# Score and value products of a pair of heads, issued head by head in turn

## The chip, the cores and the metric

The kernel runs on one core of one Trainium2 chip. The core has five engines that this text names by the short names of the profile: TensorE (PE, and PEld for its weight loads), VectorE (DVE), ScalarE (ACT), GpSimd (POOL) and SyncE (SP). Each works off its own instructions, and semaphores let one wait for another. The metric is the device time of one execution in microseconds, the median of the runs.

## The reference

Attention over 8 batches and 8 heads, 576 rows of 64 values each, keeps the 32 largest scores of each row. Its output, read as 4608 tokens of 512 values, goes through a SoLU block. All is float32.

```
scores = scale * q @ k.T                        # [8, 8, 576, 576]
kth    = the 32nd largest score of each row
attn   = softmax(scores where scores >= kth, else -1e9)
x      = (attn @ v), heads side by side         # [4608, 512]
h      = x @ w_in                               # [4608, 1024]
solu   = h * softmax(h)
ln     = (solu - mean) / sqrt(var + 1e-6) * g_ln
out    = ln @ w_out                             # [4608, 512]
```

## The kernel before

Attention runs in 32 pairs of heads, four pairs to a batch. The 576 query rows of a pair make five steps: four chunks of 128 rows, each with one tile per head, and one chunk for the two tails of 64 rows, which share a tile. So a pair has nine tiles of 128 by 576 scores.

For each step `scores` (line 206) multiplies queries with keys. Queries and keys of both heads lie in one tile `qkT` with the head dimension on the partitions, head 0 on 0 to 63 and head 1 on 64 to 127. A head's 576 columns are made in two halves of 288, in one tile `s_ps` of two PSUM banks per head, from a pool of two such tiles (`ps_big`). ScalarE scales and evicts it to `S_sb` (line 231).

`topk_softmax` finds the 32 largest on VectorE with four MAX8 and three MATCH_REPLACE8 (lines 243 and 253); ScalarE makes the exponentials `E_sb` (line 250); VectorE masks and sums them into `P_sb` (line 257); GpSimd divides by the sum (line 266). `transpose_p` turns `P_sb` on TensorE (`tp_p`, `tp_pt`, lines 277 and 280), and ScalarE copies the result to `PTm`, one tile per head for the 512 main columns, or to `PTt` for the tails.

After a pair's last step `attn_v` (line 284) multiplies values with these: into `om` (64 by 512 per head, head 0 on output partitions 0 to 63, head 1 on 64 to 127, both in one bank) and into `ot` (64 by 64 per head). Each is a sum of five products: four with `vm`, 128 rows of values, and one with `vt`, the 64 tail rows. ScalarE copies `om` to `xTm` (line 306) and `ot` to `xTt` (line 307).

When the four pairs of a batch are done, its tokens go through the SoLU block in tiles of 128: `mm1` makes `h_ps` (eight products, from `ps_big` too), `solu_ln` works on VectorE (`hmax`, line 326, first), ScalarE and GpSimd, and `mm2` transposes (`tp_ln`) and makes `o_ps`. One such piece of work is taken per step from the list `todo`. The weights come as float64 and are turned to float32 in 16 chunks in the first steps.

The order of instructions on each engine is not the order of the code: a scheduler gives each instruction a place by its inputs, its buffers and its own estimate of durations. An engine then works strictly down its list; ScalarE's list, for instance, mixes evictions, exponentials and copies. What the change moves is thus seen only in the built order.

Of the kernel before, what the change touches and what calls it, by code (L numbers as in the profile page):

```python
# [8 lines left out]
F32 = mybir.dt.float32  # L9
# [6 lines left out]
P = 128  # L16
# [2 lines left out]


def from_float64(nc, p1, p2, dst, raw):
    """dst = the nearest float32 of the float64 whose bits raw holds, in three stages.

    Bits of an integer only go through bitwise operations, or through
    arithmetic that is exact in float32: the exponent field alone, and the
    mantissa in its upper 20 and its lower 32 bits, whose sum is rounded once
    to float32. Past float32's range it gives infinity or zero.
    """
    words = raw.bitcast(U32).rearrange("p (f w) -> p f w", w=2)
    lo, hi = words[:, :, 0], words[:, :, 1]  # L30
    ex = p2.tile([P, 512], I32, tag="ln", name="w_ex")
    mi = p1.tile([P, 512], U32, tag="sq", name="w_mi")
    mant = p2.tile([P, 512], F32, tag="solu", name="w_mant")

    nc.vector.tensor_scalar(
        out=ex, in0=hi.bitcast(I32), scalar1=0x7FF00000, scalar2=None, op0=ALU.bitwise_and
    )
    nc.vector.tensor_scalar(
        out=mi, in0=hi, scalar1=0xFFFFF, scalar2=None, op0=ALU.bitwise_and
    )  # L40
    nc.gpsimd.tensor_scalar(
        out=mant, in0=mi, scalar1=2.0**-20, scalar2=1.0, op0=ALU.mult, op1=ALU.add
    )
    nc.gpsimd.tensor_scalar(
        out=ex, in0=ex, scalar1=float(-896 << 20), scalar2=0.0, op0=ALU.add, op1=ALU.max
    )
    nc.gpsimd.tensor_scalar(
        out=ex, in0=ex, scalar1=float(255 << 20), scalar2=8.0, op0=ALU.min, op1=ALU.mult
    )
    yield  # L50
    nc.vector.scalar_tensor_tensor(
        out=mant, in0=lo, scalar=2.0**-52, in1=mant, op0=ALU.mult, op1=ALU.add
    )
    nc.gpsimd.tensor_tensor(out=mant, in0=mant, in1=ex.bitcast(F32), op=ALU.mult)
    yield
    nc.vector.scalar_tensor_tensor(
        out=dst.bitcast(U32), in0=hi, scalar=0x80000000, in1=mant.bitcast(U32),
        op0=ALU.bitwise_and, op1=ALU.bitwise_or,
    )
# [3 lines left out]
def kernel(  # L63
# [7 lines left out]
    moe_g_ln: bass.AP,  # L71
    out: bass.AP,
):
    """Attention runs in pairs of heads, one batch after the other.

    A head's 576 rows are loaded as 512 main rows, row 4p + t on partition p in
    chunk t, and 64 tail rows; queries and keys keep that order throughout, and
    the stores undo it. The tails of the two heads share one tile of 128 query
    rows. The attention output is made transposed, [(head, d), token], as the
    first matrix product of the second part takes it.  # L80
    """
    nc = tc.nc
    B, H, S, D = q.shape
    NTOK, DM = out.shape
    DFF = moe_w_in.shape[1]
    NM = 4
    SM = NM * P
    ST = S - SM
# [7 lines left out]
    raw = ctx.enter_context(tc.tile_pool(name="raw", bufs=3))  # L96
# [4 lines left out]
    ps_big = ctx.enter_context(tc.tile_pool(name="ps_big", bufs=2, space=PS))  # L101
# [8 lines left out]
    w_out = const.tile([P, NF, DM], F32, tag="w_out", name="w_out")  # L110
    g_rows = const.tile([NF, P], F32, tag="g_rows", name="g_rows")
    g_col = const.tile([P, NF], F32, tag="g_col", name="g_col")

# [1 line left out]

    w_wide = moe_w_in.dtype != F32
    w_chunks = []
# [14 lines left out]
    def load_w(n):  # L132
        dst, src, _ = w_chunks[n]
        if w_wide:
            w_raw[n] = raw.tile([P, 512], mybir.dt.uint64, tag="w_raw", name="w_raw")
            dst = w_raw[n]
        nc.sync.dma_start(out=dst, in_=src)

    def finish_w(n):
        """The chunk's three stages; the next chunk's load goes ahead of the first."""  # L140
        dst, _, c = w_chunks[n]
        if n + 1 < len(w_chunks):
            load_w(n + 1)
        if w_wide:
            yield from from_float64(nc, p1, p2, dst, w_raw.pop(n))
        if c is not None:
            # ln * g @ w_out: g is per row of w_out
            nc.gpsimd.tensor_scalar(
                out=dst, in0=dst, scalar1=g_col[:, c : c + 1], scalar2=1.0,
                op0=ALU.mult, op1=ALU.mult,  # L150
            )
# [1 line left out]
    w_open = []  # L153

    def weights_step(n):
        """One stage of each open chunk, the oldest first."""
        if n < len(w_chunks):
            w_open.append(finish_w(n))
        for g in list(w_open):
            if next(g, w_open) is w_open:  # L160
                w_open.remove(g)

# [1 line left out]

    pairs = [(b, hp) for b in range(B) for hp in range(NP)]
    st = [dict() for _ in pairs]
# [2 lines left out]
    def load(i):  # L169
        b, hp = pairs[i]  # L170
        hh = slice(2 * hp, 2 * hp + 2)
        for nm, src in (("q", q), ("k", k), ("v", v)):
            # one free dimension per chunk for what the tensor engine loads as weights
            dims, order = ([P, NM, 2, D], "p t h d") if nm != "v" else ([P, 2, NM, D], "p h t d")
            m = raw.tile(dims, F32, tag=nm + "m", name=nm + "m")
            t = raw.tile([ST, 2, D], F32, tag=nm + "t", name=nm + "t")
            nc.sync.dma_start(
                out=m, in_=src[b, hh, 0:SM, :].rearrange(f"h (p t) d -> {order}", t=NM)
            )
            nc.sync.dma_start(out=t, in_=src[b, hh, SM:S, :].rearrange("h p d -> p h d"))  # L180
            st[i][nm] = (m, t)
# [25 lines left out]
        d["PTt"] = p2.tile([P, NM + 1, 2 * ST], F32, tag="PTt", name="PTt")  # L207

    def scores(i, t):
        """Score rows of query chunk t (NM: the tails), scaled, on chip."""  # L210
        d = st[i]
        qkT = d["qkT"]
        tail = t == NM
        qs = slice(SM, S) if tail else slice(t * P, (t + 1) * P)
        big = []
        for h in range(2):
            s = ps_big.tile([P, 2, 512], F32, tag="big", name="s_ps")
            hd = slice(h * D, (h + 1) * D)
            rows = slice(h * ST, (h + 1) * ST) if tail else slice(0, P)
            for half in range(2):  # L220
                nc.tensor.matmul(  # L221
                    out=s[rows, half, 0:SH], lhsT=qkT[hd, 0, qs],
                    rhs=qkT[hd, 1, half * SH : (half + 1) * SH], start=True, stop=True,
                )
            big.append((s, rows))
        d["S", t] = []
        for h, (s, rows) in enumerate(big):
            if h == 0 or not tail:
                sb = p4.tile([P, S], F32, tag="S", name="S_sb")
                d["S", t].append(sb)  # L230
            nc.scalar.activation(  # L231
                out=sb[rows, :].rearrange("p (a s) -> p a s", a=2), in_=s[rows, :, 0:SH],
                func=AF.Copy, scale=scale,
            )
# [48 lines left out]
    def attn_v(i):  # L283
        b, hp = pairs[i]
        d = st[i]
        if hp == 0:
            xs["m", b] = p2.tile([P, NP, SM], F32, tag="xTm", name="xTm")
            if b % 2 == 0:
                xs["t", b // 2] = p2.tile([P, NP, 2 * ST], F32, tag="xTt", name="xTt")
        xm, xt = xs["m", b], xs["t", b // 2]  # L290
        vm, vt = d["v"]
        om = ps_o.tile([P, 512], F32, tag="o", name="om")
        ot = ps_o.tile([P, 512], F32, tag="o", name="ot")
        for h in range(2):
            hd = slice(h * D, (h + 1) * D)
            for o, n, rhs in (
                (om, SM, d["PTm"][h]),
                (ot, ST, d["PTt"][:, :, h * ST : (h + 1) * ST]),
            ):
                for c in range(NM + 1):  # L300
                    ks = P if c < NM else ST
                    nc.tensor.matmul(  # L302
                        out=o[hd, 0:n], lhsT=vm[:, h, c, :] if c < NM else vt[:, h, :],
                        rhs=rhs[0:ks, c, :], start=(c == 0), stop=(c == NM),
                    )
        nc.scalar.copy(out=xm[:, hp, :], in_=om)  # L306
        nc.scalar.copy(out=xt[:, hp, (b % 2) * ST : (b % 2 + 1) * ST], in_=ot[:, 0:ST])
        d.clear()

# [1 line left out]

    def mm1(d, x):
        h = ps_big.tile([P, 2, 512], F32, tag="big", name="h_ps")
# [80 lines left out]
                ],  # L394
            )

# [1 line left out]

    steps = [(i, t) for i in range(len(pairs)) for t in range(NM + 1)]

# [7 lines left out]
    def behind(n):  # L408
        i, t = steps[n]
        transpose_p(i, t)  # L410
        if t == NM:
            attn_v(i)
            b, hp = pairs[i]
            if hp == NP - 1:
                queue_batch(b)

    load(0)
    load(1)
    ahead(0)
    load_g()  # L420
    load_w(0)
    for n in range(len(w_chunks) + 2):
        todo.append(lambda n=n: weights_step(n))
# [42 lines left out]
```

## Time and profile before

| | |
|---|---|
| three runs, us | 2178.75, 2178.86, 2180.56 (median 2178.86) |
| span of the profiled execution | 2181.4 us |
| its own time beside the span | none is given apart from the span |
| VectorE busy | 1910.7 us, 88% |
| TensorE busy (matmuls) | 1701.3 us, 78% |
| ScalarE busy | 813.0 us, 37% |
| GpSimd busy | 396.5 us, 18% |

The profile is of one execution; its span is 2.5 us above the median of the runs. A matmul's end is modelled, so from TensorE one reads the starts: the distance from one start to the next is what an instruction costs in a dense run. "Idle before" is the time that an engine stood still ahead of an instruction, with what ended the wait behind the arrow. Start times count from the first instruction. In the timeline neighbours of one kind are merged, with their count behind the x.

### The profile page before, as it was taken

Reading aid. Unit: us, or ns where it says so; the run is one execution under the profiler, and the core shown is the slowest. Engines: PE = TensorE matmul, PEld = TensorE weight load, DVE = VectorE, ACT = ScalarE, POOL = GpSimd, SP = SyncE. Lnnn points to the kernel's source line nnn. Section 1 sums busy time; section 2 is a strip of 40 time slices with the busy share of each in tenths; the row PEclk is TensorE's granted clock in tenths of the full one; section 3 lists DMA queues with packets and bytes.
Section 4 is the critical chain, followed back from the end, with each engine's and each line's share of the span. In section 5 each row is a group of like instructions: output and inputs, shape, how many; then the busy total and the mean of one; then the engine's idle time right before and its main releaser. Section 6 shows DMA issues by size and latency. Waiting matters only on the chain.

```text
span 2181.4 us, 20118 instructions
## 1 busy us (share of the span) xinstructions
PE 1701.3 (78%) x5761; PEld 844.0 (39%) x5761; DVE 1910.7 (88%) x4600; ACT 813.0 (37%) x1598; POOL 396.5 (18%) x475
## 2 busy tenths in 40 slices
PE   4537679786898878797787878977687987878787
PEld 2223334343343434343343434434343443344333
DVE  6889989999889998999899998899989998999931
ACT  2223334343344433443343433334334443334322
POOL 6871111111111111111111111111111110111111
PEclk9956678786798877896788977978678987789699
DMA  4210000000000000000000000000000000000000
GB/s 122 74 34 17 17 17 21 21 22 17 6 26 21 21 17 21 12 27 17 17 21 21 21 12 16 27 16 21 17 16 16 26 21 17 5 11 10 0 10 15
DMA packets 96766, 47.44 MB, mean 22 GB/s; under 512 B 81800, under 2 KB 90000, under 8 KB 96656
## 3 DMA queue, kind: packets, MB, share of 16 engines
q1 hardware_dynamic: 91408, 36.72, 6.7%
q10 hardware_dynamic: 5248, 9.44, 1.2%
q8 instruction: 46, 0.75, 0.1%
q14 instruction: 64, 0.52, 0.1%
HBM read 36.70 MB, written 9.44 MB: 21 GB/s over the span
## 4 chain that ended last, share of the span: by engine, by line
PE 55%; DVE 29%; ACT 6%; issue 6%; POOL 4%; DMA 0%; SPq 0%; POOLq 0%; ACTq 0%; DVEq 0%
PE om L302 12%; PE o_ps L365 11%; DVE rest L253 11%; PE h_ps L316 11%; DVE m L243 10%; PE s_ps L221 9%; PE tp_p L277 5%; DVE P_sb L257 5%; PE ot L302 2%; PE tp_ln L359 2%; ACT S_sb L231 2%; PE tp_qk L201 1%; POOL P_sb L266 1%; ACT PTm L278 1%; DVE solu L334 1%
## 5 line engine op out<-in xcount | busy, mean ns | idle before, releaser
L243 DVE MAX8 m<-rest 128x8 f32<-128x576 f32 x864 | 656.4, 760 | 17.1
L221 PE MATMUL s_ps<-qkT 64*128 64x288 f32 (+1 forms) x1280 | 435.8, 547 | 188.9 <-ACT S_sb L231 160.5
L266 POOL TENSOR_SCALAR P_sb<-P_sb,rden 128x576 f32<-128x576 f32 x288 | 218.0, 757 | 1564.7 <-DVE rden L265 1442.9
L277 PE MATMUL tp_p<-ident,P_sb 128*128 128x128 f32 x1152 | 243.3, 348 | 238.7 <-POOL P_sb L266 231.1
L253 DVE MATCH_REPLACE8 rest<-m,rest 128x576 f32<-128x576 f32 x576 | 427.6, 742 | 0.0
L221 PEld LDWEIGHTS s_ps<-qkT 64*128 64x128 f32 (+1 forms) x1280 | 213.5, 225 | 366.6 <-ACT S_sb L231 216.9
L277 PEld LDWEIGHTS tp_p<-ident,P_sb 128*128 128x128 f32 x1152 | 162.3, 174 | 400.6 <-POOL P_sb L266 301.2
L231 ACT ACTIVATE S_sb<-s_ps 128x576 f32<-128x576 f32 (+1 forms) x320 | 204.6, 650 | 299.2 <-PE s_ps L221 134.3
L278 ACT COPY PTm<-tp_p 128x512 f32<-128x512 f32 x256 | 149.9, 586 | 399.5 <-PE tp_p L277 399.5
L365 PE MATMUL o_ps<-w_out,lnT 128*128 128x512 f32 x576 | 278.4, 640 | 3.3 <-ACT lnT L362 3.3
L257 DVE SCALAR_TENSOR_TENSOR P_sb<-S_sb,m,E_sb 128x576 f32<-128x576 f32 x288 | 233.6, 811 | 47.9 <-ACT E_sb L250 46.5
L250 ACT ACTIVATE E_sb<-S_sb,nmax 128x576 f32<-128x576 f32 x288 | 222.3, 772 | 123.2 <-DVE nmax L246 122.6
L302 PE MATMUL om<-PTm,vm 128*64 128x512 f32 x512 | 242.7, 608 | 1.5 <-ACT PTm L278 1.5
L316 PE MATMUL h_ps<-w_in,xTm 128*128 128x512 f32 x512 | 236.3, 603 | 4.0 <-ACT S_sb L231 2.8
L243 DVE MAX8 m<-S_sb 128x8 f32<-128x576 f32 x288 | 213.9, 743 | 16.0 <-ACT S_sb L231 16.0
L253 DVE MATCH_REPLACE8 rest<-m,S_sb 128x576 f32<-128x576 f32 x288 | 213.9, 743 | 0.0
L365 PEld LDWEIGHTS o_ps<-w_out,lnT 128*128 128x128 f32 x576 | 115.8, 206 | 146.1 <-issue 134.5
L326 DVE TENSOR_REDUCE hmax<-h_ps 128x1 f32<-128x1024 f32 x36 | 44.0, 1221 | 124.5 <-PE h_ps L316 124.5
L316 PEld LDWEIGHTS h_ps<-w_in,xTm 128*128 128x128 f32 x512 | 92.7, 192 | 104.6 <-issue 95.5
L302 PEld LDWEIGHTS om<-PTm,vm 128*64 128x64 f32 x512 | 63.5, 138 | 139.5 <-issue 123.7
L280 PE MATMUL tp_pt<-ident,P_sb 128*64 128x128 f32 x288 | 97.8, 339 | 0.0
L306 ACT COPY xTm<-om 128x512 f32<-128x512 f32 x32 | 18.7, 585 | 197.1 <-PE om L302 197.1
(66 smaller groups left out, 1319.0 us busy)
## 6 DMA issues: line engine op xcount, KB each, us to landing
qm<-in_q_dram SPq DMA_DIRECT2D x32, 256.0 KB, 3.7
km<-in_k_dram SPq DMA_DIRECT2D x32, 256.0 KB, 3.9
vm<-in_v_dram SPq DMA_DIRECT2D x32, 256.0 KB, 2.7
out_dram<-osb ACTq DMA_DIRECT2D x32, 256.0 KB, 2.2
w_raw<-in_moe_w_in_dram SPq DMA_DIRECT2D x8, 512.0 KB, 3.9
w_raw<-in_moe_w_out_dram SPq DMA_DIRECT2D x8, 512.0 KB, 3.4
qt<-in_q_dram SPq DMA_DIRECT2D x32, 32.0 KB, 2.2
kt<-in_k_dram SPq DMA_DIRECT2D x32, 32.0 KB, 2.3
```

Source lines behind the costliest of these rows:

```text
L221: nc.tensor.matmul(out=s[rows, half, 0:SH], lhsT=qkT[hd, 0, qs], rhs=qkT[hd, 1, half * SH : (half + 1) * SH], start=True, stop=True,)
L231: nc.scalar.activation(out=sb[rows, :].rearrange("p (a s) -> p a s", a=2), in_=s[rows, :, 0:SH], func=AF.Copy, scale=scale,)
L243: nc.vector.max(m, cur)
L250: nc.scalar.activation(out=e, in_=sb, func=AF.Exp, bias=nmax)
L253: nc.vector.match_replace(nxt, m, cur, NEG)
L257: nc.vector.scalar_tensor_tensor(out=pt, in0=sb, scalar=m[:, 7:8], in1=e, op0=ALU.is_ge, op1=ALU.mult, accum_out=den,)
L266: nc.gpsimd.tensor_scalar(out=pt, in0=pt, scalar1=rden, scalar2=1.0, op0=ALU.mult, op1=ALU.mult)
L277: nc.tensor.transpose(tp[:, c, :], pt[:, c * P : (c + 1) * P], ident)
L278: nc.scalar.copy(out=dst[:, 0:NM, :], in_=tp)
L302: nc.tensor.matmul(out=o[hd, 0:n], lhsT=vm[:, h, c, :] if c < NM else vt[:, h, :], rhs=rhs[0:ks, c, :], start=(c == 0), stop=(c == NM),)
L316: nc.tensor.matmul(out=h[:, half, :], lhsT=x[:, c, :], rhs=w_in[:, c, half * 512 : (half + 1) * 512], start=(c == 0), stop=(c == NP - 1),)
L365: nc.tensor.matmul(out=o, lhsT=lnT[:, c, :], rhs=w_out[:, c, :], start=(c == 0), stop=(c == NF - 1),)
```

## The change

In `scores` both heads' tiles are taken first; then the loop over the halves is the outer one and the loop over the heads the inner one. In `attn_v` the loop over the heads becomes the innermost: `om` of both heads first, product by product in turn, then `ot`. The number, the sizes and the operands of the products stay. The remaining lines of the diff replace comments by blank lines. Line numbers from `scores` on differ by one or two between the kernels (the value product is line 302 before and line 301 after).

```diff
         big = []
         for h in range(2):
-            s = ps_big.tile([P, 2, 512], F32, tag="big", name="s_ps")
-            hd = slice(h * D, (h + 1) * D)
             rows = slice(h * ST, (h + 1) * ST) if tail else slice(0, P)
-            for half in range(2):
+            big.append((ps_big.tile([P, 2, 512], F32, tag="big", name="s_ps"), rows))
+
+        for half in range(2):
+            for h, (s, rows) in enumerate(big):
+                hd = slice(h * D, (h + 1) * D)
                 nc.tensor.matmul(
                     out=s[rows, half, 0:SH], lhsT=qkT[hd, 0, qs],
                     rhs=qkT[hd, 1, half * SH : (half + 1) * SH], start=True, stop=True,
                 )
-            big.append((s, rows))
...
-        for h in range(2):
-            hd = slice(h * D, (h + 1) * D)
-            for o, n, rhs in (
-                (om, SM, d["PTm"][h]),
-                (ot, ST, d["PTt"][:, :, h * ST : (h + 1) * ST]),
-            ):
-                for c in range(NM + 1):
-                    ks = P if c < NM else ST
+
+        for o, n in ((om, SM), (ot, ST)):
+            for c in range(NM + 1):
+                ks = P if c < NM else ST
+                for h in range(2):
+                    rhs = d["PTm"][h] if n == SM else d["PTt"][:, :, h * ST : (h + 1) * ST]
                     nc.tensor.matmul(
-                        out=o[hd, 0:n], lhsT=vm[:, h, c, :] if c < NM else vt[:, h, :],
+                        out=o[h * D : (h + 1) * D, 0:n],
+                        lhsT=vm[:, h, c, :] if c < NM else vt[:, h, :],
                         rhs=rhs[0:ks, c, :], start=(c == 0), stop=(c == NM),
                     )
```

Since a scheduler places the instructions, the lists of all engines move. Three places are shown, each of before and of the change. Numbers in names are running numbers of tiles; `PTm0` and `PTm1` are the transposed attention of the two heads; sizes are partitions by columns of the output.

TensorE at the end of the third batch's last pair, about 804 to 821 us in the trace of before; first before:

```order
L302 MATMUL om_5830<-PTm0_5256,vm_4337 64x512 x4
L277 MATMUL tp_p_5740<-ident_82,P_sb_5651 128x128 x4
L280 MATMUL tp_pt_5746<-ident_82,P_sb_5651 64x128
L302 MATMUL om_5830<-PTm0_5256,vt_4338 64x512
L302 MATMUL om_5830<-PTm1_5257,vm_4337 64x512 x4
L302 MATMUL om_5830<-PTm1_5257,vt_4338 64x512
L316 MATMUL h_ps_5854<-w_in_89,xTm_4410 128x512 x5
L277 MATMUL tp_p_5821<-ident_82,P_sb_5724 128x128 x4
L280 MATMUL tp_pt_5827<-ident_82,P_sb_5724 64x128
L316 MATMUL h_ps_5854<-w_in_89,xTm_4410 128x512
L302 MATMUL ot_5831<-PTt_5258,vm_4337 64x64 x4
L302 MATMUL ot_5831<-PTt_5258,vt_4338 64x64
```

The same place in the changed kernel, from the first value product on:

```order
L301 MATMUL om_5830<-PTm0_5256,vm_4337 64x512
L316 MATMUL h_ps_5854<-w_in_89,xTm_4410 128x512 x2
L278 MATMUL tp_p_5740<-ident_82,P_sb_5651 128x128 x4
L281 MATMUL tp_pt_5746<-ident_82,P_sb_5651 64x128
L316 MATMUL h_ps_5854<-w_in_89,xTm_4410 128x512
L301 MATMUL om_5830<-PTm1_5257,vm_4337 64x512
L301 MATMUL om_5830<-PTm0_5256,vm_4337 64x512
L301 MATMUL om_5830<-PTm1_5257,vm_4337 64x512
```

And, after three more `om` rows of the same kind, from the last product with `vm` on:

```order
L301 MATMUL om_5830<-PTm1_5257,vm_4337 64x512
L301 MATMUL om_5830<-PTm0_5256,vt_4338 64x512
L301 MATMUL om_5830<-PTm1_5257,vt_4338 64x512
L223 MATMUL s_ps_5863<-qkT_5676 128x288 x2
L278 MATMUL tp_p_5821<-ident_82,P_sb_5724 128x128 x4
L281 MATMUL tp_pt_5827<-ident_82,P_sb_5724 64x128
L316 MATMUL h_ps_5854<-w_in_89,xTm_4410 128x512
L301 MATMUL ot_5831<-PTt_5258,vm_4337 64x64 x8
L301 MATMUL ot_5831<-PTt_5258,vt_4338 64x64 x2
L316 MATMUL h_ps_5854<-w_in_89,xTm_4410 128x512 x4
```

Head 0's five `om` products and head 1's five stood as two blocks; now one product of head 0 stands alone, and the other nine alternate behind the transposes of head 1. Three of the eight `h_ps` products stand ahead of them, and one head's scores (`s_ps_5863`) ahead of the tails' transposes. The `ot` products of both heads stand together by `vm` and `vt`.

VectorE at that batch's end, around the first operation that reads the new `h_ps`; before:

```order
L253 MATCH_REPLACE rest_5802<-m8_5796,S_sb_5704 128x576
L262 TENSOR_SCALAR rden_5792<-den_5790 128x1
L326 TENSOR_REDUCE hmax_5941<-h_ps_5854 128x1
L265 RECIPROCAL rden_5792<-rden_5792 128x1
L243 MAX m8_5804<-rest_5802 128x8
L253 MATCH_REPLACE rest_5806<-m8_5804,rest_5802 128x576
L330 TENSOR_SCALAR rs_5944<-rs_5944 128x1
L243 MAX m8_5808<-rest_5806 128x8
```

And in the changed kernel:

```order
L254 MATCH_REPLACE rest_5802<-m8_5796,S_sb_5704 128x576
L263 TENSOR_SCALAR rden_5792<-den_5790 128x1
L244 MAX m8_5804<-rest_5802 128x8
L266 RECIPROCAL rden_5792<-rden_5792 128x1
L254 MATCH_REPLACE rest_5806<-m8_5804,rest_5802 128x576
L244 MAX m8_5808<-rest_5806 128x8
L326 TENSOR_REDUCE hmax_5941<-h_ps_5854 128x1
L254 MATCH_REPLACE rest_5810<-m8_5808,rest_5806 128x576
```

`hmax_5941` stood behind `rden_5792`; now two MAX and one MATCH_REPLACE of the running top-k stand ahead of it, and the operations that follow from it come later.

ScalarE at the end of the batch's second pair, about 701 to 708 us in the trace of before; before:

```order
L231 ACTIVATE S_sb_4849<-s_ps_4844 128x576
L306 COPY xTm_4410<-om_4910 128x512
L307 COPY xTt_4411<-ot_4911 128x64
L342 ACTIVATE sq_4945,var_4946<-solu_4941,nmu_4942 128x1024
L231 ACTIVATE S_sb_4959<-s_ps_4953 128x576
L231 ACTIVATE S_sb_4961<-s_ps_4956 128x576
L250 ACTIVATE E_sb_4967<-S_sb_4847,nmax_4965 128x576
```

And in the changed kernel:

```order
L232 ACTIVATE S_sb_4849<-s_ps_4842 128x576
L342 ACTIVATE sq_4945,var_4946<-solu_4941,nmu_4942 128x1024
L306 COPY xTm_4410<-om_4910 128x512
L307 COPY xTt_4411<-ot_4911 128x64
L251 ACTIVATE E_sb_4967<-S_sb_4847,nmax_4965 128x576
L232 ACTIVATE S_sb_4959<-s_ps_4953 128x576
L232 ACTIVATE S_sb_4961<-s_ps_4954 128x576
```

The exponential `E_sb_4967` stood behind `sq_4945` and two evictions of scores; now it follows the copies of `om` and `ot` directly, and `sq_4945` has gone ahead of these.

## Rows read from the trace of the kernel before

**Rows 1.** The page, busy time, share of the span and instructions of each engine.

```profile
PE 1701.3 (78%) x5761; PEld 844.0 (39%) x5761; DVE 1910.7 (88%) x4600; ACT 813.0 (37%) x1598; POOL 396.5 (18%) x475
```

**Rows 2.** Waits of VectorE, 300 to 2080 us: total, times, longest (us).

```profile
DVE hmax L326 <- PE h_ps L316: 73.7, 24, 6.0
DVE P_sb L257 <- ACT E_sb L250: 45.9, 37, 3.6
```

**Rows 3.** Timeline, VectorE, one batch: start us, us, what [idle before, releaser].

```profile
627.29 0.82 DVE L257 SCALAR_TENSOR_TENSOR P_sb<-S_sb,m,E_sb 128x576 f32<-128x576 f32 x1 [1.10 <-ACT E_sb L250]
...
647.28 1.23 DVE L326 TENSOR_REDUCE hmax<-h_ps 128x1 f32<-128x1024 f32 x1 [2.55 <-PE h_ps L316]
...
708.34 0.98 DVE L257 SCALAR_TENSOR_TENSOR P_sb<-S_sb,m,E_sb 128x576 f32<-128x576 f32 x1 [3.03 <-ACT E_sb L250]
...
771.63 0.82 DVE L257 SCALAR_TENSOR_TENSOR P_sb<-S_sb,m,E_sb 128x576 f32<-128x576 f32 x1 [2.57 <-ACT E_sb L250]
...
823.46 1.23 DVE L326 TENSOR_REDUCE hmax<-h_ps 128x1 f32<-128x1024 f32 x1 [5.97 <-PE h_ps L316]
...
824.67 0.74 DVE L243 MAX8 m<-rest 128x8 f32<-128x576 f32 x1
```

**Rows 4.** Timeline, TensorE, 803.9 to 823.5 us.

```profile
803.97 3.65 PE L302 MATMUL om<-PTm,vm 128*64 128x512 f32 x8
807.55 0.66 PE L277 MATMUL tp_p<-ident,P_sb 128*128 128x128 f32 x4
...
808.24 1.07 PE L302 MATMUL om<-PTm,vt 64*64 64x512 f32 x2
809.24 3.65 PE L302 MATMUL om<-PTm,vm 128*64 128x512 f32 x8
812.82 1.07 PE L302 MATMUL om<-PTm,vt 64*64 64x512 f32 x2
813.82 4.56 PE L316 MATMUL h_ps<-w_in,xTm 128*128 128x512 f32 x10
818.21 0.60 PE L277 MATMUL tp_p<-ident,P_sb 128*128 128x128 f32 x4
...
819.71 0.68 PE L302 MATMUL ot<-PTt,vm 128*64 128x64 f32 x8
...
821.44 1.98 PE L316 MATMUL h_ps<-w_in,xTm 128*128 128x512 f32 x4
823.36 0.51 PE L221 MATMUL s_ps<-qkT 64*128 64x288 f32 x1
```

**Rows 5.** Timeline, ScalarE, 704 to 708.6 us.

```profile
704.30 0.59 ACT L306 COPY xTm<-om 128x512 f32<-128x512 f32 x1 [8.51 <-PE om L302]
...
705.27 1.15 ACT L342 ACTIVATE sq<-solu,nmu 128x1024 f32<-128x1024 f32 x1
...
707.47 0.78 ACT L250 ACTIVATE E_sb<-S_sb,nmax 128x576 f32<-128x576 f32 x1
```

**Rows 6.** Timeline, TensorE, score products, 690 to 710 us.

```profile
691.01 1.24 PE L221 MATMUL s_ps<-qkT 64*128 64x288 f32 x4
...
705.06 1.25 PE L221 MATMUL s_ps<-qkT 64*128 64x288 f32 x8
```

**Rows 7.** Line 302: count, duration ns min/median/max, first and last start.

```profile
L302 PEld LDWEIGHTS om<-PTm,vm x512: 132/137/232, 94.8 to 2089.4; 128*64 128x64 f32 x171
L302 PE MATMUL om<-PTm,vm x512: 592/592/1116, 94.8 to 2089.9; 128*64 128x512 f32 x171
```

**Rows 8.** Timeline, GpSimd, 800 to 826 us.

```profile
805.68 0.74 POOL L266 TENSOR_SCALAR P_sb<-P_sb,rden 128x576 f32<-128x576 f32 x1 [5.53 <-DVE rden L265]
811.95 0.74 POOL L266 TENSOR_SCALAR P_sb<-P_sb,rden 128x576 f32<-128x576 f32 x1 [5.53 <-DVE rden L265]
```

**Rows 9.** Timeline, GpSimd, the last batch.

```profile
2083.52 0.74 POOL L266 TENSOR_SCALAR P_sb<-P_sb,rden 128x576 f32<-128x576 f32 x1 [5.53 <-DVE rden L265]
```

**Rows 10.** Stretch of rows 4: length, busy us (x), granted clock, DMA share, GB/s.

```profile
799.40:823.40 24.00, 24.00 (x88) 0.92 0.12 29
```

## The prediction, made before the changed kernel ran

> **What bounds the kernel now.** Start with the busy shares [rows 1]: VectorE works 1910.7 us of a span of 2181.4 us, TensorE 1701.3. VectorE alone could not end before 1911 us; what can be won lies in the 271 us in which it does not work. I read its waits next, from 300 to 2080 us (behind the weights, ahead of the end). Two lines hold nearly all [rows 2]: 73.7 us for `h_ps`, the first product of the second part, and 45.9 us for `E_sb`, the exponentials, which ScalarE makes.
>
> The timeline of VectorE gives the places [rows 3]. In one batch, from 560 to 825 us, five waits matter: 1.10 us for `E_sb` (at 627.29), 2.55 for `h_ps` (647.28), 3.03 for `E_sb` (708.34), 2.57 for `E_sb` (771.63), 5.97 for `h_ps` (823.46). Together 15.2 us. Seven batches end between 300 and 2080 us, so this pattern makes 106 of the 120 us of rows 2.
>
> What do the five have in common? Ahead of the last, TensorE is busy without a pause from 803.97 to 823.36 us [rows 4]: value products, half of the SoLU product, the tails' value products, the rest of `h_ps`. The value products take 9.16 us of it as `om` (803.97 to 807.55 and 808.24 to 813.82) and 1.73 us as `ot` (819.71 to 821.44). The 3.03 us are lost on ScalarE [rows 5]: it sits 8.51 us in front of the copy `xTm<-om`, waiting for the last value product, and the exponential that VectorE wants comes behind it, at 707.47, in a queue that is worked off in order. Value products stand ahead of the other three in the same way.
>
> **The change, part by part.** The trace counts two instructions per float32 product, the order counts products.
>
> *Score products.* The heads use rows 0 to 63 and 64 to 127 of the array. Do they overlap? The trace of before shows it [rows 6]: four instructions of one head take 1.24 us (691.01), eight of both heads 1.25 us (705.06). With the heads next to each other the array already runs them together, without alternation. In the order 85 of 160 chunks had their heads adjacent; now 69 are alternated, 3 adjacent and 88 apart, since each head's tile waits for a buffer of its own. I cost this part at nothing: adjacent ones overlapped before, and those that are apart still are.
>
> *Value products.* Both heads use all 128 rows, with different columns (outputs on partitions 0 to 63 and 64 to 127). The trace of before never shows two of them side by side: between the heads always stood a `vt` product of 64 rows, and a change of row count costs time. Eight `vm` instructions take 3.58 us (809.24 to 812.82), 0.447 each; the two of `vt` take 1.00 (812.82 to 813.82), so up to 0.11 is the change [rows 4]. The unknown is bounded from both sides. Low: the heads overlap as the scores do, each pair of products for the time of one. High: each change of head exposes a weight load of 137 ns and the 145 ns by which a matmul's record (592) outlasts 447 [rows 7], 0.28 us, 18 times per pair of heads. I take the low end, to which rows 6 are nearest: same type, same engine, other strips of the array.
>
> The Trainium skill, page "TensorE: Matmul & The Clock Gate", section "Part 3: Packing small matmuls", says that a weight load overlaps running matmuls only where the row group differs. By that rule the value products would not pair well, which is the second rival below; no row here shows two column strips at work. The same section gives three column tiles 2.38 times the speed of one, which would put the sum at its low end. And it has matmuls start and end in strict order; rows 6, eight in the time of four, agree with its packing.
>
> *At the batch's end* I take the new order of TensorE with the durations of rows 4 and 6: one `om` 0.89, two `h_ps` 1.76, transposes 0.69, `h_ps` 0.88, nine `om` in pairs 4.58 (four times 0.89, and 1.00), one head's scores 1.16, transposes 0.69, `h_ps` 0.88, `ot` in pairs 0.87, four `h_ps` 3.51. That is 15.9 us instead of 19.4. The transposes don't wait longer: GpSimd has their inputs done at 806.4 and 812.7 [rows 8]. On VectorE `hmax` now stands behind two MAX and a MATCH_REPLACE more, 2.2 us of ready work at 0.74 each (824.67 in rows 3). 3.5 + 2.2 = 5.7 of the 5.97 us go.
>
> *At 708* `om` and `ot` shrink by 9.16 - 0.89 - 4.58 + 0.87 = 4.6 us (the first product stands alone), and the exponential no longer has `sq` and two evictions ahead of it on ScalarE. The 3.03 go. *At 771* all ten products pair: 4.58 + 0.87 instead of 10.9, and 5.4 is more than 2.57. *At 627* eviction and exponential move ahead of `xTm` on ScalarE: 1.10 go. *At 647* TensorE's chain starts up to 4.6 us sooner, against 2.55.
>
> *Sum.* 106 us are open. The waits at 771 and their like differ from batch to batch, and a VectorE that runs earlier meets the next thing that is late; I keep 85%, 90 us. In the last batch the second head's input comes from GpSimd at 2084.3 [rows 9] whatever TensorE does; only what lies behind it shrinks, 0 to 2 us, I take 1. At the start VectorE's operations on the 16 weight chunks trade places with a MAX or MATCH_REPLACE of 0.74 us: at most 12 us either way, taken as nothing, since the neighbours are ready work. 2181.4 - 91 = 2090 us for the profiled execution, whose span is the only time shown for it; the median of the three runs is 2.5 us less than that span, so **2088 us**.
>
> **The rivals.**
>
> *No overlap in the columns, and no harm.* For it: no row shows any. Against it: rows 6. Then only the moved places work. At the batch's end nine `om` cost 8.1 and `ot` 1.6: 20.2 us on TensorE, 0.8 more than before, 2.2 covered by `hmax`'s new place, 1.4 won. The 1.10 go; at 708 the exponential comes 2.2 us sooner (`sq` at 705.27, exponential at 707.47); at 771 0.3 is won, at 647 0.5 lost. 4.5 us a batch, 31 in all: about 2148 us.
>
> *Each change of head costs.* The place is the alternating run of `om` and `ot`, the price a weight load that can't hide and a drain. The 4.5 us of the case above are used up at 4.5 / (4 places x 18 changes) = 0.06 us a change; from there on the kernel is slower. At 0.11, the change of rows, a batch loses 3.4 us: 2203. At 0.28 it loses 15.7: 2289. For it: no row shows a load for one head under the other's matmul. Against: one head's loads hide behind its own matmuls now.
>
> *The pairs run at the lower clock.* In the stretch of rows 4 the granted clock is 0.92 [rows 10], nearly all at 2.4 GHz. A TensorE with half the value work could be granted 1.2 GHz there; then a pair costs what two cost now, and the four `h_ps` and the scores behind them double as well, 4.7 us a batch, against the 4.5 that the order gives: no change, 2180. Against it: the same 16 us stay without a pause.
>
> **How the numbers follow.** Forecast 70%, with a range of its own from 2060 (all 106 us and some of the other 13) to 2125 (half of them); no overlap 17%; cost per change 8%; lower clock 5%. A measurement of this kernel can tell about 0.2%, 4.4 us, from no change. So faster 87%, same 5%, slower 8%. The range for 8 in 10 starts at 2060 and reaches to 2155, over the second case with its spread; beyond it lie the last two and a small part of the forecast.
>
> **What would show it.** Right: in the alternating run, eight `vm` instructions in about 1.9 us instead of 3.58; the wait ahead of `hmax` at a batch's end under 1 us; the two lines of rows 2 together under 45 us; score products of one chunk as long as before; VectorE's busy time unchanged. Wrong: the `vm` instructions still 0.43 us or more apart at full clock, which is the first or the second rival by the size of the gap; or a granted clock near half in that run, which is the third. If pairs overlap and the waits stay, the step that fails is that value products end them.

## The result, and the profile after

The changed kernel takes 2075.6 us (four runs, 2074.1 to 2076.7) beside 2179.7 us before in the same comparison: a ratio of 0.952, 95% interval 0.9506 to 0.9533. The span of its profiled execution is 2073.2 us, 108.2 less than before.

The page's busy line, beside [rows 1]:

```profile
PE 1552.6 (75%) x5761; PEld 783.8 (38%) x5761; DVE 1903.7 (92%) x4600; ACT 819.1 (40%) x1598; POOL 399.6 (19%) x475
```

VectorE works nearly as long as before (7.0 us less), TensorE 148.7 us less. What VectorE waits for between 300 and 1975 us (the last batch's end, which began at 2080 before, now begins there); total, times, longest, beside [rows 2]:

```profile
DVE hmax L326 <- PE h_ps L316: 21.7, 19, 3.1
DVE m L244 <- ACT S_sb L232: 3.6, 4, 1.0
DVE P_sb L258 <- ACT E_sb L251: 0.8, 2, 0.4
```

The two lines of rows 2 go from 119.6 to 22.5 us, which is 97 of the 108. TensorE at the end of the third batch, beside [rows 4], from its timeline:

```profile
772.46 1.24 PE L301 MATMUL om<-PTm,vm 128*64 128x512 f32 x2
773.63 1.99 PE L316 MATMUL h_ps<-w_in,xTm 128*128 128x512 f32 x4
...
776.95 3.65 PE L301 MATMUL om<-PTm,vm 128*64 128x512 f32 x14
780.52 1.08 PE L301 MATMUL om<-PTm,vt 64*64 64x512 f32 x4
781.53 1.23 PE L223 MATMUL s_ps<-qkT 64*128 64x288 f32 x4
...
784.25 0.69 PE L301 MATMUL ot<-PTt,vm 128*64 128x64 f32 x16
784.87 0.33 PE L301 MATMUL ot<-PTt,vt 64*64 64x64 f32 x4
785.13 3.70 PE L316 MATMUL h_ps<-w_in,xTm 128*128 128x512 f32 x8
788.76 1.23 PE L223 MATMUL s_ps<-qkT 64*128 64x288 f32 x4
```

Fourteen `vm` instructions start within 3.57 us (776.95 to 780.52), where eight took 3.58: the columns of the two heads work side by side. From the first `om` to the last `h_ps` it is 16.3 us instead of 19.4. VectorE's waits for it, from its timeline, beside [rows 3]:

```profile
622.20 1.22 DVE L326 TENSOR_REDUCE hmax<-h_ps 128x1 f32<-128x1024 f32 x1 [0.59 <-PE h_ps L316]
...
788.87 1.23 DVE L326 TENSOR_REDUCE hmax<-h_ps 128x1 f32<-128x1024 f32 x1 [1.33 <-PE h_ps L316]
...
1105.24 1.23 DVE L326 TENSOR_REDUCE hmax<-h_ps 128x1 f32<-128x1024 f32 x1 [3.05 <-PE h_ps L316]
```

5.97 at the batch's end became 1.33, the 2.55 of [rows 3] became 0.59. The last row is new: two places (1105 and 1586 us) wait 3.05 us. On ScalarE, beside [rows 5], the copy of `om` finds its data there and the exponential follows at once:

```profile
674.64 1.15 ACT L342 ACTIVATE sq<-solu,nmu 128x1024 f32<-128x1024 f32 x1 [3.22 <-DVE nmu L337]
...
675.78 0.56 ACT L306 COPY xTm<-om 128x512 f32<-128x512 f32 x1
...
676.36 0.78 ACT L251 ACTIVATE E_sb<-S_sb,nmax 128x576 f32<-128x576 f32 x1
```

So nearly every sign that the prediction asked for is there. The wait at a batch's end was to be under 1 us: over the seven batches it is 0.33 to 1.33 us, and 1.08 and 1.33 are over. Whether the prediction's reason is the reason is another matter: the pairs became shorter, and the order of all engines changed at the same time. The experiments take these apart.

### The profile page after: what moved, and what is told of

Its sections match the earlier page's. It is cut to its first block, busy times and chain, and to the rows that moved or that the text cites. A ratio compares the mean times of both kernels' runs of the same rounds, so it can differ in the third digit from the quotient of the medians.

```text
span 2073.2 us, 20096 instructions
## 1 busy us (share of the span) xinstructions
PE 1552.6 (75%) x5761; PEld 783.8 (38%) x5761; DVE 1903.7 (92%) x4600; ACT 819.1 (40%) x1598; POOL 399.6 (19%) x475
## 4 chain that ended last, share of the span: by engine, by line
PE 47%; DVE 36%; issue 7%; ACT 5%; POOL 4%; SPq 0%; DMA 0%; ACTq 0%; POOLq 0%; DVEq 0%
DVE rest L254 14%; DVE m L244 12%; PE o_ps L365 11%; PE h_ps L316 11%; PE s_ps L223 9%; PE om L301 6%; DVE P_sb L258 6%; PE tp_p L278 5%; PE tp_ln L359 2%; PE tp_qk L201 1%; POOL P_sb L267 1%; ACT S_sb L232 1%; DVE hmax L326 1%; ACT PTm L279 1%; POOL w_ex L47 1%
## 5 line engine op out<-in xcount | busy, mean ns | idle before, releaser
L223 PE MATMUL s_ps<-qkT 64*128 64x288 f32 (+1 forms) x1280 | 426.6, 550 | 212.8 <-ACT S_sb L232 198.8
L223 PEld LDWEIGHTS s_ps<-qkT 64*128 64x128 f32 (+1 forms) x1280 | 206.4, 226 | 392.2 <-ACT S_sb L232 258.9
L301 PE MATMUL om<-PTm,vm 128*64 128x512 f32 x512 | 158.6, 643 | 5.3 <-ACT PTm L279 5.3
L301 PEld LDWEIGHTS om<-PTm,vm 128*64 128x64 f32 x512 | 41.4, 145 | 91.1 <-issue 74.9
L359 PE MATMUL tp_ln<-ident,ln 128*128 128x128 f32 x288 | 55.0, 353 | 18.0 <-POOL ln L349 10.1
```

What stands on the lines that cost most here:

```text
L223: nc.tensor.matmul(out=s[rows, half, 0:SH], lhsT=qkT[hd, 0, qs], rhs=qkT[hd, 1, half * SH : (half + 1) * SH], start=True, stop=True,)
L301: nc.tensor.matmul(out=o[h * D : (h + 1) * D, 0:n], lhsT=vm[:, h, c, :] if c < NM else vt[:, h, :], rhs=rhs[0:ks, c, :], start=(c == 0), s ...
```

## The experiments

All ratios are to the kernel before, run beside. "Theory 1" below is the prediction's: the value products became shorter, and that is the gain.

**Which half of the change.** One kernel has the new `attn_v` with the old `scores`, one the new `scores` with the old `attn_v`.

> Only the value products alternate between the heads; the score products go head by head, as before the change. Theory (all the gain comes from the value products): 2076 us, within 5, and the four score products of a step take the 1.24 us that they take in both kernels. Rival (alternating the scores brings part of it): 2090 us or more.

> Only the score products alternate; the value products go head by head, as before the change. Theory (the heads' score products overlap in either order): 2179 us, within 5, and VectorE's waits for hmax at a batch's end stay near 6 us. Rival (alternating the scores brings part of it): 2165 us or less.

Value products alone: 2070.5 us, ratio 0.9492 (0.9476 to 0.9508). Scores alone: 2173.5, ratio 0.9964 (0.9951 to 0.9977). The value products carry the gain. Both results lie half a microsecond below the range that was expected: alternating the scores brought 7 us alone and cost about 5 in company. It shortens no product (four instructions of one head take 1.23 us, as before), so these few microseconds are likely to come from the order of the rest; no run shows their places.

**No room side by side.** Each value product takes both heads' values as 128 columns:

```diff
-                        out=o[h * D : (h + 1) * D, 0:n],
-                        lhsT=vm[:, h, c, :] if c < NM else vt[:, h, :],
-                        rhs=rhs[0:ks, c, :], start=(c == 0), stop=(c == NM),
+                        out=o[:, 0:n],
+                        lhsT=(vm[:, c, :, :] if c < NM else vt).rearrange("p h d -> p (h d)"),
+                        rhs=rhs[0:ks, c, :], start=(c == 0 and h == 0), stop=(c == NM and h == 1),
```

> The changed order, but each value product takes the values of both heads as 128 columns and writes all 128 rows of the result, added up over both heads, so that no two products can stand in the array side by side (what the value products compute is changed by this, and the values are loaded in pieces of 256 bytes in place of 1 KB). Theory (the gain is mostly the two heads running side by side): eight products with all rows take 3.5 us or more, as head by head, and only what the order gives is left, 2140 to 2180 us. Rival (the gain is the order: om complete ahead of ot, fewer changes of the number of rows): under 2110 us.

2077.4 us, ratio 0.9524 (0.951 to 0.9538), as fast as the change, although no two value products ran side by side. TensorE at the third batch's end, from its timeline:

```profile
773.06 4.45 PE L301 MATMUL om<-PTm,vm 128*128 128x512 f32 x10
777.35 0.60 PE L278 MATMUL tp_p<-ident,P_sb 128*128 128x128 f32 x4
...
779.71 1.98 PE L301 MATMUL om<-PTm,vt 64*128 64x512 f32 x4
781.62 2.00 PE L301 MATMUL ot<-PTt,vm 128*128 128x64 f32 x16
```

Ten instructions need 4.29 us to the next start, 0.43 each. This went against theory 1, and theory 2 took shape: the new order alone is the gain.

**The same order, no room.** To separate the two, the changed kernel's order was held fast: a table ties each instruction to the one before it on its engine, and both heads' products with `vm` write the same columns.

```diff
-                        out=o[h * D : (h + 1) * D, 0:n],
+                        out=o[0:D, 0:n] if c < NM else o[h * D : (h + 1) * D, 0:n],
...
+    for eng, text in ORDER.items():
+        raw = zlib.decompress(base64.b85decode(text))
+        place = [k + x for k, (x,) in enumerate(struct.iter_unpack("<h", raw))]
+        for a, b in zip(place, place[1:]):
+            tc.add_manual_dep(ins[eng][b], ins[eng][a].name, info, reason="order")
```

> Every engine issues its instructions in exactly the order of the changed kernel (a table at the end of the kernel ties each instruction to the one before it), but both heads' om and ot products with vm write the same 64 rows of the result, so that they use the same columns of the array and cannot run side by side (what the value products compute is changed by this). Theory 1 (the gain needs the two heads side by side): om and ot take 4.3 us more at a batch's end, the wait for hmax there grows from about 1 to about 5 us and the others grow too, 2120 to 2150 us. Theory 2 (the new order is the gain, as the run with 128 columns suggests): under 2095 us.

2137.2 us, ratio 0.9801 (0.9785 to 0.9818): theory 2 falls. In this order the products side by side are worth 62 us. VectorE's waits (300 to 1975 us), and TensorE's long run at the third batch's end:

```profile
DVE hmax L377 <- PE h_ps L367: 55.3, 20, 3.8
DVE P_sb L309 <- ACT E_sb L302: 21.8, 10, 3.5
```

```profile
795.90 6.22 PE L352 MATMUL om<-PTm,vm 128*64 128x512 f32 x14
802.05 1.08 PE L352 MATMUL om<-PTm,vt 64*64 64x512 f32 x4
```

6.15 us for the fourteen, where the change needs 3.57, and the waits come back. By the names that the traces keep, the instructions of VectorE, ScalarE, GpSimd and TensorE stand in the same order in both, so the order is not what differs. The changed kernel was not run tied to its own order; that ties by themselves cost little is seen below, where a kernel tied in the same way takes 2071 us.

**One place moved.** In the kernel before, `hmax` is tied behind the last MAX of the step in which its piece of work is taken.

```diff
+                mark[0] = nc.vector.max(m, cur)
...
+        with tc.issue_after(mark[0].ins):
+            nc.vector.tensor_reduce(out=nmax, in_=h, axis=AX.X, op=ALU.max, negate=True)
```

> The kernel before, in which hmax is issued behind the last MAX of its step: behind 8 of the step's 8 MAX at a batch's end instead of 5, and instead of 6 and 3 at the two other places; the products stay head by head. Theory 2 (where hmax stands on VectorE is what counts): the waits for hmax between 300 and 2080 us fall from 73.7 us to under 20, the waits for E_sb stay, 2110 to 2135 us. Theory 1 (VectorE only meets the late value products at the next place): the waits move to E_sb and S_sb, over 2150 us.

2168.3 us, ratio 0.9937 (0.9922 to 0.9952). The expectation misjudged the place: that step is the next one, so `hmax` came eleven MAX later and not three (at the third batch's end; two to eleven elsewhere). Its waits are gone, and others grew:

```profile
DVE P_sb L259 <- ACT E_sb L252: 75.3, 44, 5.0
DVE rs L333 <- ACT e_sb L332: 22.2, 17, 2.8
DVE m L245 <- ACT S_sb L231: 5.7, 7, 0.9
```

This is theory 1's picture: one instruction moved out of the way only meets the next thing that is late. It is no test of a shorter move: `hmax` alone four MAX later, where the orders below have it, was not run. The same edit on value products alternated and scores head by head:

> Value products alternated, scores head by head, and hmax issued behind the last MAX of its step. Both theories: the 20 us of waits for hmax between 300 and 1975 us that are left go, among them five of 3.06 us, 2045 to 2062 us. If the waits move to the next thing that is late instead: 2066 us or more.

2083.4 us, ratio 0.9549 (0.9535 to 0.9563): slower than without it by some 13 us. The `hmax` waits are gone (four of them had been of about 3.06 us, not five), but VectorE is busy 1915.0 us instead of 1903.6, and waits for `S_sb` and `e_sb` grew to 22 us.

**Blocks.** How near must the heads' products stand? In blocks of four and of two:

```diff
-            for c in range(NM + 1):
-                ks = P if c < NM else ST
-                for h in range(2):
+            for h, c in [(h, c) for cs in (range(NM), (NM,)) for h in range(2) for c in cs]:
+                    ks = P if c < NM else ST
```

(for two, `cs in ((0, 1), (2, 3), (NM,))`.)

> om and ot one after the other as in the change, but within each the products stand in blocks: four of head 0, four of head 1, then the two tails with 64 rows. Theory A (the heads run side by side where their blocks are neighbours with the same rows, as the score products did before the change): 2076 to 2100 us, eight products in about 1.9 us. Theory B (only products that stand next to each other in the order run side by side): eight products in about 3.1 to 3.6 us, one pair of them overlapping at the seam, and 2135 to 2180 us.

> As in the run with blocks of four products, but with blocks of two: head 0's first two chunks, head 1's first two, then the same for the last two, then the tails. Theory A (the array takes a product of the other head early when it is at most about four instructions away, as the seams of the blocks of four suggest): all pairs run side by side, sixteen instructions in about 3.7 us, 2065 to 2090 us. Theory B (only the seam of two blocks overlaps): sixteen instructions in 5.3 us or more, over 2105 us.

Four: 2123.8 us, ratio 0.974 (0.9725 to 0.9755). Two: 2112.9, one run. Sixteen instructions of a pair whose inputs are all there, first in blocks of four, then of two, from TensorE's timeline:

```profile
747.40 5.42 PE L300 MATMUL om<-PTm,vm 128*64 128x512 f32 x16
752.75 1.08 PE L300 MATMUL om<-PTm,vt 64*64 64x512 f32 x4
```

```profile
745.36 3.71 PE L300 MATMUL om<-PTm,vm 128*64 128x512 f32 x16
749.00 1.08 PE L300 MATMUL om<-PTm,vt 64*64 64x512 f32 x4
```

5.35 and 3.64 us. With blocks of four only the seam overlaps, two products of each head: 2.7 us for eight instructions, between the 1.9 of theory A and the 3.1 to 3.6 of theory B, and 2123.8 us lies between their ranges too, so both missed. Blocks of two (four instructions) run fully side by side, as theory A said, as the two halves of a head's scores do in [rows 6]. But its time is 37 us above the change with the same array time here: theory A was right on the array and wrong on the kernel. It has another order, and it lost the clock in places (last section); the two were not taken apart.

**Order and array.** Theory 3 puts the two together. The scheduler places by its own estimate. How many MAX stand on VectorE ahead of the `hmax` of the third batch's end (`hmax_5941` of the order shown above), and what it waits there:

| kernel | products of the two heads | MAX ahead | wait, us | time, us |
|---|---|---|---|---|
| before | one after the other | 437 | 5.97 | 2180 |
| changed | side by side | 439 | 1.33 | 2076 |
| changed, order held | one after the other | 439 | 3.37 | 2137 |
| 128 columns | one after the other | 441 | 0.79 | 2077 |

When the outputs leave no room side by side, the scheduler puts `hmax` four MAX later than in the kernel before. The operations and their number are the same, so its estimate seems to count the heads of the kernel before as overlapping, by their columns, while the array ran blocks of five products one after the other. The loss would then be an order made for products that were shorter than the real ones, and there are two ways out: shorten the products, or mend the order. First the variant with the same columns, with the scheduler free:

> The changed kernel, but both heads' om and ot products with vm write the same 64 rows of the result, so that they cannot run side by side (what the value products compute is changed by this), and the scheduler, which sees this, orders the instructions anew: at a batch's end hmax then stands two MAX later than in the change, elsewhere two later. Theory 3 (the loss of the kernel before is an order made as if the heads ran side by side, on an array that ran them one after the other; the gain comes when order and array agree): 2072 to 2095 us, although TensorE's value products take as long as before. Theory 1 (the shorter value products are the gain): 2130 to 2150 us, as with the pinned order.

2068.8 us, ratio 0.9489 (0.9472 to 0.9506), with the `vm` products serial, 3 us under theory 3's range. Its waits (300 to 1975 us):

```profile
DVE rs L330 <- ACT e_sb L329: 4.7, 11, 0.5
DVE hmax L326 <- PE h_ps L316: 4.5, 6, 1.4
```

Held in the changed kernel's order these products gave 2137; in the order made for them, 68 us less. Then the kernel before itself, no line of its arithmetic changed, in a foreign order:

> The kernel before, its products head by head with the reference's result, but every engine issues in an order that the scheduler made for a kernel whose heads cannot run side by side (tied by a table). Theory 3: 2075 to 2100 us, the two lines of waits together under 40 us, without any alternation of the products. Theory 1: value products as long as before keep most of the waits, over 2140 us.

2107.6 us, ratio 0.9662 (0.9648 to 0.9676), between the two ranges, although `hmax` now stands four MAX later, as in the table's last row, and waits little. Its waits (300 to 1975 us):

```profile
DVE rs L381 <- ACT e_sb L380: 30.8, 14, 2.2
DVE P_sb L308 <- ACT E_sb L301: 18.7, 11, 3.2
DVE hmax L377 <- PE h_ps L367: 11.2, 18, 1.0
```

The order came from a kernel in which the `vt` products, on different columns, may still have looked to the scheduler as if they overlapped. Without that (the 37 us of the expectation are counted from the kernel with the new `attn_v` alone; over the changed kernel it is 32):

> As the run with the kernel before in another order, but the order is now one that the scheduler made for a kernel in which none of the value products of the two heads can run side by side, those with vt among them (before, only those with vm). The products stay head by head, with the reference's result. If the 37 us that are left over the changed kernel come from the scheduler's remaining misjudgement of the vt products: 2070 to 2095 us, and the waits for e_sb of 2.2 us are gone. If they come from what alternation does to the order besides (om complete ahead of ot): 2100 to 2112 us.

2071.3 us, ratio 0.9505 (0.9489 to 0.9521). The whole gain, head by head. Beside the run at 2107.6 us, GpSimd has the same order and VectorE too, but for three `hmax` that stand one MAX later; so nearly all of the 36 us between the two lie in the orders of TensorE and ScalarE. The page's busy line, then VectorE's waits from 300 to 1975 us:

```profile
PE 1646.6 (80%) x5761; PEld 816.7 (39%) x5761; DVE 1904.7 (92%) x4600; ACT 816.0 (39%) x1598; POOL 393.9 (19%) x475
```

```profile
DVE rs L381 <- ACT e_sb L380: 11.3, 14, 0.8
DVE hmax L377 <- PE h_ps L367: 8.3, 13, 1.3
DVE m L294 <- ACT S_sb L282: 4.4, 6, 1.4
```

TensorE at the third batch's end, from its timeline, and VectorE's at the place where it meets it:

```profile
767.87 3.65 PE L353 MATMUL om<-PTm,vm 128*64 128x512 f32 x8
...
773.14 3.65 PE L353 MATMUL om<-PTm,vm 128*64 128x512 f32 x8
776.72 1.07 PE L353 MATMUL om<-PTm,vt 64*64 64x512 f32 x2
...
779.27 0.68 PE L353 MATMUL ot<-PTt,vm 128*64 128x64 f32 x8
...
781.00 6.28 PE L367 MATMUL h_ps<-w_in,xTm 128*128 128x512 f32 x14
787.21 1.23 PE L272 MATMUL s_ps<-qkT 64*128 64x288 f32 x4
```

```profile
784.95 0.74 DVE L294 MAX8 m<-S_sb 128x8 f32<-128x576 f32 x1
785.60 0.80 DVE L308 SCALAR_TENSOR_TENSOR P_sb<-S_sb,m,E_sb 128x576 f32<-128x576 f32 x1
...
787.32 1.23 DVE L377 TENSOR_REDUCE hmax<-h_ps 128x1 f32<-128x1024 f32 x1
```

From the first `om` to the last `h_ps` it is 19.3 us (767.87 to 787.21), as in [rows 4]; yet `hmax` loses nothing, because VectorE has 4 MAX and what belongs to them to do first. So a chain of this length need not cost the 5.97 us; in the kernel before, VectorE had been sent to the end of it too early. VectorE's order is only a part of the loss, though: the run at 2107.6 us has `hmax` at the same place.

Last, both at once: alternated value products in an order made for serial ones.

> Value products alternated and side by side, scores head by head, but issued in the order that the scheduler made for products that cannot run side by side, so that VectorE reaches hmax two MAX later than the array now needs. Both theories: the waits for hmax of 3.06 us and the small ones at the batches' ends go, 15 to 20 us, 2050 to 2060 us. If the order without the five early waits costs the same elsewhere: 2066 us or more.

2071.9 us, ratio 0.9498 (0.9484 to 0.9512): no better than either. The waits left between 300 and 1975 us add up to 26 us here and to 24 in the run above; the small differences among the runs from 2069 to 2077 were not followed. Of the kernels that compute the reference, the one with the new `attn_v` and the old `scores` is the quickest, 2070.5 us, no clear step ahead of the 2071.3 of the kernel before in its mended order.

## Why the prediction came out

*Scores at nothing.* Right: no product got shorter, and without this part the kernel is no slower.

*Value products pair in columns.* Right, at the low end that was chosen: fourteen in 3.57 us. The Trainium skill, page "TensorE: Matmul & The Clock Gate", section "Part 3: Packing small matmuls", lets a weight load overlap only under another row group; here both heads use the same 128 rows, and the fourteen (three pairs of products and one alone, so eight turns) take 0.446 us a turn, the 0.447 of a single product's instruction in [rows 4]. The measurement decides.

*The batch's end.* 15.9 us were worked out, 16.3 measured; of 5.97 us, 4.64 went instead of 5.7. *At 647* 2.55 became 0.59, *at 708* the exponential stands free. *Sum.* The two lines lost 97 us; 90 were expected. The 85% that I kept was the mis-sized term: the waits that came in place of the old ones are smaller. The list of five waits also left out a sixth of like size, 2.50 us for `h_ps` at 607.97; over the seven batches its kind fell from 12.0 to 6.4 us. And a third line of waits, which the sum did not count, went altogether; in the kernel before, 300 to 2080 us:

```profile
DVE rs L330 <- ACT e_sb L329: 6.4, 17, 0.9
```

VectorE's records also shrank by 7.0 us (1910.7 to 1903.7), which I had taken as unchanged; a record behind a wait can be longer, as the 0.98 us of the one at 708.34 in [rows 3], and that is a part of it. The start and the end of the program moved by a few microseconds and no more.

*The rivals.* The first, no overlap, only moved places, was priced at 2148 us; the run with the order held, which is nearly that case (its products with `vt` still pair), took 2137. Between the case and the forecast lay 60 us; the pairs were worth 62 in this order. So the arithmetic on both sides of the forecast was sound for this order. The second, a price for each change of head, is refuted by the 3.57 us. The third, the lower clock, did happen, in a few places; see the last section.

*What the argument missed.* The step that says that TensorE's chain is too long and that value products end the five waits names only one of two ways out. With the chain as long as before and an order that fits it, the time is the same. The rows could not tell this: an instruction that waits 5.97 us looks alike whether its input is late or it stands too early in its queue. The prediction treated the moved `hmax` as worth 2.2 us of ready work; four MAX further would have been worth all of it, with the other engines placed to match (the run at 2107.6 us shows what it is worth without that). That the scheduler's estimate counts overlapping columns is inferred from the orders that it made and from the last runs, not read from its numbers.

## What to carry to other kernels

Ahead of making a late producer faster, ask whether its reader stands in the right place: where VectorE is the bound and always has ready work, a producer on a less busy engine costs nothing if the order knows its true duration. A scheduler's order is only as good as its estimate, so look for places where its view of overlap and the array's differ, and either write the products so that they overlap as it expects (alternate them: blocks of two overlapped as well, but that kernel took 2113 us), or give it the order. Moving `hmax` alone by two to eleven MAX did not do it, and VectorE's fitting order with less fitting ones on TensorE and ScalarE brought two thirds of the gain (2107.6 us); the other queues have to move along.

## What the runs showed of the hardware

Two float32 products with the same 128 rows and different columns run fully side by side, also in blocks of two products; in blocks of four only the seam does (5.35 us for sixteen instructions, against 3.64). So TensorE, unlike what is said of engines ahead of the prediction, does not start everything strictly down its list: in blocks of two, four instructions of head 0 stand ahead of head 1's first, and those of one head start 0.43 us apart; started down the list, sixteen would take over 5 us by this estimate, and they take 3.64.

The run of value products was sometimes granted half the clock. In the changed kernel, ahead of the wait of 3.05 us at 1105, TensorE's timeline and then the stretch 1079.4 to 1084.2 us (columns as in [rows 10], with the busy time of each engine):

```profile
1078.25 6.21 PE L301 MATMUL om<-PTm,vm 128*64 128x512 f32 x14
1084.39 1.08 PE L301 MATMUL om<-PTm,vt 64*64 64x512 f32 x4
```

```profile
1079.40:1084.20 4.80, 4.80 (x12) 1.09 (x8) 4.70 (x14) 1.31 (x2) 2.00 (x2) 0.58 0.00 0
```

The granted clock is 0.58, most of it at 1.2 GHz, and the fourteen take 6.14 us instead of 3.57: 2.57 lost, and the wait for `hmax` behind it is 3.05 where the same place of another batch waits 0.59. The alternated kernel with head-by-head scores has four such places. In the blocks of two it stands behind each of the seven batch ends, in the next batch's first pair; one of them:

```profile
607.68 6.17 PE L300 MATMUL om<-PTm,vm 128*64 128x512 f32 x12
```

```profile
607.60:612.80 5.20, 5.20 (x11) 1.48 (x11) 5.10 (x15) 0.00 (x0) 2.69 (x4) 0.50 0.01 3
```

Products side by side are not needed for it. The run with the order held, whose `vm` products are serial, has it behind four of the seven batch ends, 8.70 us for fourteen instead of 6.15:

```profile
607.75 8.77 PE L352 MATMUL om<-PTm,vm 128*64 128x512 f32 x14
616.45 1.07 PE L352 MATMUL om<-PTm,vt 64*64 64x512 f32 x4
```

So some 5 of the 62 us between that run and the change may be the clock's (four drops of 2.55 us against two of 2.57). What sets it off was not tried. In the 15 us before the clock fell in the changed kernel, at about 1076 us, TensorE had no pause longer than 0.74 us. From 300 to 1975 us the granted clock was 0.80 in the changed kernel, 0.81 in the run with the order held, 0.82 in the kernel before and 0.85 in the kernel before in its mended order; how much of this the products side by side make is not shown.
